# A bilinear feed-forward layer behind a gated linear attention: the second product of pairs of token groups in seven block products instead of eight

## The chip, the cores and the metric

The kernel runs on one core of a Trainium2 chip. The metric is the time on the device in microseconds: the median of three runs, and beside it one profiled execution, whose trace is what the rows below come from. Engines go by the profile's names: PE multiplies matrices (PEld is its loading of weights), DVE and ACT work element by element and can read PSUM, where PE leaves its results, POOL does so in SBUF alone, and SP issues DMAs.

## The reference

Two stages follow each other, all in float32. The first is a recurrence over 768 positions for each of 4 batches x 8 heads, with a head dimension of 48; the second takes its result as 3072 tokens of 384 numbers.

```python
f = 1.0 / (1.0 + np.exp(-f_logit))
for t in range(S):
    state = f[:, :, t, :, None] * state + np.einsum('bhd,bhe->bhde', k[:, :, t], v[:, :, t])
    y[:, :, t] = np.einsum('bhd,bhde->bhe', q[:, :, t], state)
x = y.transpose(0, 2, 1, 3).reshape(B * S, H * D)
a = x @ w_a                  # 3072x384 @ 384x1536
b = x @ w_b
return (a * b @ w_out)       # 3072x1536 @ 1536x384
```

## The kernel before

The work is cut into 8 blocks of 384 tokens, two to a batch. The attention for a block comes as two units of four heads (16 units, `u`), the layer for a block as twelve steps `up` and six steps `down`.

A unit goes through stages that touch several engines. `front(u)` (lines 229 to 256) is ACT's two sigmoids, then DVE's scans over the positions, then the reciprocals, more scans and the products that scale q and k. `scores` (275) is 48 small matmuls on PE and a masked copy by DVE to `at`; `turn` (302) transposes k on PE, and ACT copies the result; `gains` (317) is up to 48 small matmuls, and then DVE's chain of six additions and two scalings that makes the states `st`; `within` (354) and `across` (372) are PE's contributions to the unit's result, which ACT copies to `y` and SP sends into `xT`, the token block in the layout that `up` reads, as five DMAs (line 410). Behind them `across` issues the loads of unit u+3. `slot(u)` (467) strings these together in six stages, with `front(u+1)` between them, so that units overlap.

`up(blk, ft)` (419) makes 128 of the 1536 columns of a and of b for a block: three matmuls each of a 128x128 weight with 384 tokens (L425). `product()` (434) then has ACT copy b to SBUF (L440), and DVE multiply a and b into a tile `ab` (L442). The prologue leaves a product behind by one step, so that it always stands behind the next `up`. `down(blk, part)` (447) is half of the second product for a group of 128 tokens: six of twelve matmuls of a 128x128 piece of ab with 384 columns of `w_out` (L453) into one bank of PSUM; the second half ends with ACT's copy to `o_sb` (L463) and a DMA to the output (L465). PSUM's pool `ps_f` has four banks, which ups and downs share; the attention has its own.

Each engine executes its instructions in the order in which the program writes them. That order is set by the loop at lines 609 to 622: `rest` lists the ups and downs (blocks 0 and 1 are interleaved, later blocks are twelve ups and then six downs), and beside it `queue` holds the stages of the slots with the step at which each is due (lines 602 to 608). A stage that is due is written between the matmuls of a step and its product. In the early steps `end` and `begin` also convert weights that arrive as float64 (lines 169 to 218); `w_out` comes last, and then DVE has no more of that to do.

PE takes a float32 matmul as two records of load and matmul each, so 288 matmuls of L453 show as 576.

Of the kernel before, what the change touches and what calls it, by code (L numbers as in the profile page):

```python
# [10 lines left out]
FP32 = mybir.dt.float32  # L11
# [5 lines left out]
ALU = mybir.AluOpType  # L17
# [3 lines left out]
BLK = 384  # L21
PIECE = 768
# [56 lines left out]
def by_quotients(ctx, tc, q, k, f_logit, v, moe_w_a, moe_w_b, moe_w_out, out, ident, weights, bad):  # L79
# [17 lines left out]
    ab_pool = ctx.enter_context(tc.tile_pool(name="ab", bufs=2 * NFT))  # L97
# [4 lines left out]
    def fixed(shape, name):  # L102
        return fixedp.tile(shape, FP32, tag=name, name=name)
# [198 lines left out]
    def turn(u, spare=False):  # L302

        kf = halves(sets[u % NSET]["k"])
        kT = sb1.tile([128, 2, NC, 128], FP32, tag="kT", name="kT")
        ps = pair(spare)
        for n in range(2):
            for c in range(NC):
                o = n * BLK + c * C
                nc.tensor.transpose(ps[n][:, c * C:c * C + C], kf[:, o:o + C], ident)  # L310
            if spare:
                nc.scalar.copy(kT[:, n].rearrange("s c x -> s (c x)"), ps[n][:, 0:BLK])
        if not spare:
            nc.scalar.copy(kT.rearrange("s n c x -> s n (c x)"), ps_x[:, :, 0:BLK])  # L314
        live[u]["kT"] = kT
# [97 lines left out]
        if u >= NQ:  # L413
            load_unit(u + NSET)

    products = {blk: [] for blk in range(NBLK)}
    factors = []

    def up(blk, ft):

        x, ps = xT[blk], {}
        for nm, w in (("b", w_b), ("a", w_a)):
            ps[nm] = ps_f.tile([128, 512], FP32, tag="f", name="f")[:, 0:BLK]
            for kt in range(NKT):
                nc.tensor.matmul(  # L425
                    ps[nm],
                    lhsT=w[:, kt, ft * 128:ft * 128 + 128],
                    rhs=x[:, kt],
                    start=kt == 0,
                    stop=kt == NKT - 1,  # L430
                )
        factors.append((blk, ps))

    def product():

        if not factors:
            return
        blk, ps = factors.pop(0)
        b_sb = sb2.tile([128, BLK], FP32, tag="b_sb", name="b_sb")
        nc.scalar.copy(b_sb, ps["b"])  # L440
        ab = ab_pool.tile([128, BLK], FP32, tag="ab", name="ab")
        nc.vector.tensor_tensor(ab, ps["a"], b_sb, ALU.mult)  # L442
        products[blk].append(ab)

    results = []

    def down(blk, part):

        tg, half = divmod(part, 2)
        if half == 0:  # L450
            results.append(ps_f.tile([128, 512], FP32, tag="f", name="f")[:, 0:DM])
        for ft in range(half * NFT // 2, (half + 1) * NFT // 2):
            nc.tensor.matmul(  # L453
                results[-1],
                lhsT=products[blk][ft][:, tg * 128:tg * 128 + 128],
                rhs=w_out[:, ft],
                start=ft == 0,
                stop=ft == NFT - 1,
            )
        if half == 0:  # L460
            return
        o_sb = sb2.tile([128, DM], FP32, tag="o_sb", name="o_sb")
        nc.scalar.copy(o_sb, results.pop())  # L463
        r0 = blk * BLK + tg * 128
        nc.sync.dma_start(out=out[r0:r0 + 128], in_=o_sb)  # L465
# [24 lines left out]
    def check_held():  # L490

        n = NU * 3
        fits = fixed([128, NU], "fits")
        some = fixed([128, 2], "some")
# [4 lines left out]
        ps = ps_x  # L499
        nc.tensor.matmul(ps[0:1, 0, 0:1], lhsT=some[:, 0:1], rhs=ones, start=True, stop=True)  # L500
        nc.vector.tensor_scalar(bad, ps[0:1, 0, 0:1], 128.0 * n, None, ALU.is_lt)

    with tc.manual_schedule():
        nc.scalar.preload_act_table_set("sigmoid_and_others")
# [91 lines left out]
        rest += [(down, blk, part) for blk in range(2) for part in range(2 * NTG)]  # L596
        for blk in range(2, NBLK):
            rest += [(up, blk, ft) for ft in range(NFT)] + [(down, blk, part) for part in range(2 * NTG)]
        slots = {s: slot(s) for s in range(2 * NQ, NU + 1)}
        a_block = NFT + 2 * NTG  # L600

        queue = [(2 * NFT - 4 + d, fronts[2 * NQ]) for d in (0, 0.9, 1.8)]
        for s in slots:
            at, pace = (s - 2 * NQ - 2) * a_block / 2 + 2 * a_block - (7 if s < NU else 8.5), 1
            if s < 3 * NQ + 1:
                at, pace = 2 * NFT - 2 + 4.7 * (s - 2 * NQ), 0.5
            queue += [(at + pace * d, slots[s]) for d in (0, 1.2, 2.6, 4, 5.5, 7)]
        queue.sort(reverse=True, key=lambda x: x[0])
        for step, (what, blk, i) in enumerate(rest, 5):
            if what is up:  # L610
                convert(needed(i))
                up(blk, i)
            while queue and queue[-1][0] <= step:
                next(queue.pop()[1], None)
            end(6 + (step - 4))
            product()
            begin(ended[0] + 2)
            if what is down:
                product()
                down(blk, i)  # L620
            if (what, blk, i) == (down, NBLK - 2, 2 * NTG - 1):
                check_held()
        for _, s in reversed(queue):
            next(s, None)
# [357 lines left out]
```

## Time and profile before

| what | us |
|---|---|
| median of three runs | 675.97 |
| lowest and highest of them | 674.87, 677.78 |
| the profiled execution | 675.24 |
| its span, first to last instruction | 673.4 |
| PE busy in the span | 633.0 |
| DVE, ACT, POOL busy | 257.2, 174.3, 66.9 |
| PE in the second product (L453) | 191.0 |
| PE in the two first products (L425) | 203.6 + 204.4 |

A row of a group gives the line, the engine, the operation, out<-in by the program's names, the partitions and elements, and the number of records; behind the first bar the busy time in all and the mean of one in ns, behind the second the idle time of the engine just before them and what ended it. A row of the timeline begins with its start and its length in us. A record of a matmul includes the way through the array, so that records of a stream overlap: their distance, not their length, is what a stream costs.

### The profile page before, as it was taken

The numbers are of one execution on the slowest core, as the hardware profiler recorded it, in microseconds if no ns is written. First come the engines' busy times: TensorE is split into PE (matmuls) and PEld (weight loads), VectorE is DVE, ScalarE is ACT, GpSimd is POOL, SyncE is SP. The second block draws the span as 40 slices with busy tenths as digits, with TensorE's granted clock in tenths as the row PEclk, the third lists the DMA queues.
The fourth block names the chain that finished last, engine by engine and source line by source line (L and its number), as shares of the span: only waits on it lengthen the run. The fifth ranks groups of instructions, "written<-read, shape, count | busy, mean of one in ns | idle before, by whom it ended". The sixth has DMA issues, their size and how long they took to land.

```text
span 673.4 us, 11228 instructions
## 1 busy us (share of the span) xinstructions
PE 633.0 (94%) x4770; PEld 386.6 (57%) x4770; DVE 257.2 (38%) x498; ACT 174.3 (26%) x300; POOL 66.9 (10%) x57
## 2 busy tenths in 40 slices
PE   1577999999999999999999999999999999999996
PEld 1454555556665666656665666556666566555553
DVE  7978899864423143222413125042523111001100
ACT  3565578410221211112211212112121111111100
POOL 6234356110000000000000000000000000000000
PEclk9877999999999999999999999999999999999999
DMA  8698746000134003140303003040031000010000
GB/s 202 169 239 244 207 128 221 1 1 13 37 99 101 1 19 72 33 92 0 89 14 86 28 0 90 23 100 2 21 73 34 16 0 20 19 36 0 1 13 27
DMA packets 30204, 43.29 MB, mean 64 GB/s; under 512 B 3776, under 2 KB 24768, under 8 KB 30144
## 3 DMA queue, kind: packets, MB, share of 16 engines
q1 hardware_dynamic: 29856, 42.19, 23.9%
q8 instruction: 39, 0.64, 0.4%
q10 hardware_dynamic: 288, 0.30, 0.2%
q14 instruction: 21, 0.17, 0.1%
HBM read 33.03 MB, written 4.72 MB: 56 GB/s over the span
## 4 chain that ended last, share of the span: by engine, by line
PE 87%; DVE 4%; DMA 4%; SPq 1%; issue 1%; ACT 1%; POOL 0%; DVEq 0%; ACTq 0%
PE f L425 54%; PE f L453 26%; DMA xT<-y 2%; DMA k_in<-in_k_dram 2%; PE ps_y L363 2%; PE ps_x L283 2%; PE ps_y L384 1%; PE ps_x L329 1%; DVE inv L252 1%; PE ps_x L310 1%; SPq L410 1%; DVE f_in L242 1%; ACT y L396 1%; DMA f_in<-in_f_logit_dram 0%; DVE k_in L254 0%
## 5 line engine op out<-in xcount | busy, mean ns | idle before, releaser
L425 PE MATMUL f<-xT,w_a 128*128 128x384 f32 x576 | 203.6, 490 | 5.6 <-DVE start L247 4.6
L425 PE MATMUL f<-xT,w_b 128*128 128x384 f32 x576 | 204.4, 490 | 2.5 <-DMA xT<-y 2.1
L453 PE MATMUL f<-w_out,ab 128*128 128x384 f32 x576 | 191.0, 489 | 0.0
L425 PEld LDWEIGHTS f<-xT,w_a 128*128 128x128 f32 x576 | 110.1, 191 | 83.2 <-issue 6.4
L425 PEld LDWEIGHTS f<-xT,w_b 128*128 128x128 f32 x576 | 107.3, 190 | 75.8 <-issue 4.4
L453 PEld LDWEIGHTS f<-w_out,ab 128*128 128x128 f32 x576 | 107.7, 190 | 71.8
L442 DVE TENSOR_TENSOR ab<-f,b_sb 128x384 f32<-128x384 f32 x96 | 53.2, 555 | 179.1 <-PE f L425 145.5
L440 ACT COPY b_sb<-f 128x384 f32<-128x384 f32 x96 | 46.0, 479 | 206.7 <-PE f L425 205.8
L237 POOL TENSOR_SCALAR inv<-inv 128x768 f32<-128x768 f32 x16 | 15.4, 959 | 367.8 <-ACT inv L234 367.8
L463 ACT COPY o_sb<-f 128x384 f32<-128x384 f32 x24 | 11.5, 479 | 151.5 <-PE f L453 141.1
L185 POOL TENSOR_SCALAR h<-h 128x768 f32<-128x768 f32 (+1 forms) x20 | 43.0, 2152 | 58.9 <-ACT h L179 58.9
L345 DVE TENSOR_TENSOR st<-st,ps_x 128x96 f32<-128x96 f32 x80 | 20.3, 253 | 63.5 <-PE ps_x L329 47.2
L396 ACT COPY y<-ps_y 48x384 f32<-48x384 f32 (+1 forms) x45 | 21.4, 475 | 66.7 <-PE ps_y L384 63.8
L283 PE MATMUL ps_x<-q_in,k_in 48*64 48x64 f32 x720 | 15.6, 236 | 22.3 <-DVE k_in L254 22.3
L299 DVE TENSOR_TENSOR at<-ps_x,causal 128x768 f32<-128x768 f32 x15 | 14.4, 958 | 57.4 <-PE ps_x L283 57.4
L242 DVE TENSOR_TENSOR_SCAN f_in<-f_in,zero 128x384 f32<-128x384 f32 x32 | 28.8, 942 | 8.7 <-ACT f_in L235 5.4
L283 PEld LDWEIGHTS ps_x<-q_in,k_in 48*64 48x64 f32 x720 | 14.0, 150 | 24.1 <-POOL causal L528 14.1
L252 DVE TENSOR_TENSOR_SCAN inv<-inv,start,zero 128x128 f32<-128x128 f32 x64 | 26.9, 462 | 0.0
L343 DVE COPY st<-ps_x 128x96 f32<-128x96 f32 x8 | 2.0, 256 | 51.4 <-PE ps_x L329 51.4
L314 ACT COPY kT<-ps_x 128x768 f32<-128x768 f32 x12 | 9.6, 798 | 41.7 <-PE ps_x L310 41.7
L182 ACT ACTIVATE bit<-sign 128x768 uint16<-128x768 bf16 (+1 forms) x20 | 19.7, 985 | 0.8
L179 ACT ACTIVATE h<-raw 128x768 f32<-128x768 f32 (+1 forms) x20 | 16.9, 846 | 3.6 <-issue 1.9
(64 smaller groups left out, 304.2 us busy)
## 6 DMA issues: line engine op xcount, KB each, us to landing
f_in<-in_f_logit_dram SPq DMA_DIRECT2D x32, 144.0 KB, 3.1
k_in<-in_k_dram SPq DMA_DIRECT2D x32, 144.0 KB, 3.5
q_in<-in_q_dram SPq DMA_DIRECT2D x32, 144.0 KB, 4.1
v_in<-in_v_dram SPq DMA_DIRECT2D x16, 288.0 KB, 4.5
raw<-in_moe_w_out_dram SPq DMA_DIRECT2D x6, 768.0 KB, 4.4
out_dram<-o_sb SPq DMA_DIRECT2D x24, 192.0 KB, 1.9
raw<-in_moe_w_b_dram SPq DMA_DIRECT2D x5, 768.0 KB, 6.3
raw<-in_moe_w_a_dram SPq DMA_DIRECT2D x5, 768.0 KB, 6.5
```

Source lines behind the costliest of these rows:

```text
L179: nc.scalar.activation(h, hi.bitcast(FP32), AF.Abs, scale=HI_SCALE)
L182: nc.scalar.activation(bit.bitcast(U16).rearrange("p (n two) -> p n two", two=2)[:, :, 1], sgn, AF.Relu, scale=-32768.0)
L185: nc.gpsimd.tensor_scalar(h, h, HI_MAX, None, ALU.min)
L242: nc.vector.tensor_tensor_scan(x[:, c], x[:, c], none, math.exp(MIDDLE), ALU.mult, ALU.add)
L252: nc.vector.tensor_tensor_scan(inv[:, w], inv[:, w], none[:, 0:C], first, ALU.mult, ALU.add)
L283: nc.tensor.matmul(ps[h][SUB * p:SUB * p + SUB, o:o + SUB], lhsT=kf[r, tokens(n, c, p)], rhs=qf[r, tokens(n, c, p)], start=True, stop=True,)
L345: nc.vector.tensor_tensor(st[:, j], before, new, ALU.add)
L396: nc.scalar.copy(y[r:r + rows, :, p], ps[p][e:e + rows, 0:BLK].rearrange("r (o m) -> r o m", m=SUB))
L425: nc.tensor.matmul(ps[nm], lhsT=w[:, kt, ft * 128:ft * 128 + 128], rhs=x[:, kt], start=kt == 0, stop=kt == NKT - 1,)
L440: nc.scalar.copy(b_sb, ps["b"])
L442: nc.vector.tensor_tensor(ab, ps["a"], b_sb, ALU.mult)
L453: nc.tensor.matmul(results[-1], lhsT=products[blk][ft][:, tg * 128:tg * 128 + 128], rhs=w_out[:, ft], start=ft == 0, stop=ft == NFT - 1,)
```

## The change

The 128-token groups of a batch are taken in three pairs: groups 0 and 1 of the even block, its group 2 with group 0 of the odd block, and groups 1 and 2 of the odd block. For a pair, the second product is seen as a product of two matrices of 2x2 blocks: rows are the two groups, the inner dimension of 1536 is cut in two halves of six 128-blocks, and the 384 columns in two halves of 192. It is made by Winograd's form of Strassen's method, seven products of blocks and a number of sums in place of eight products. Four combinations of blocks of `w_out` (t1 to t4) are made once, by DVE, when `w_out` has been converted. Each pair makes four sums of blocks of ab (s1 to s4) on DVE, in tiles that the conversion used before, seven products on PE (P1 to P7, in the order of the code), copies of two partial results on ACT, and five sums of 192 columns with PSUM on DVE. Two results of 192 columns share a bank (x0 and x1, m0 and m1), and waits are kept by tile, so the next writer of one half also waits for the reader of the other.

The tiles `ab` now hold six 128-blocks for the three groups of a block, four tiles in all. A pair's first sum, s3, is written ahead, between earlier steps. The stages of the units are written between the seven products as well, a product counting half a step; their due times are new numbers; `across` moves from behind `gains` to behind `turn`; and the sums of the check on the input (`check_held`) are split off and written ahead.

```diff
     def down(pair):
...
+        s3 = add(block(), a11, a21, ALU.subtract)
+        yield
+        x, m = (ps_f.tile([128, 512], FP32, tag="f", name="f") for _ in range(2))
+        x0, x1, m0, m1 = (t[:, HM * i:HM * i + HM] for t in (x, m) for i in range(2))
+        times(x0, a11, b11, True)
+        u2 = sb2.tile([128, HM], FP32, tag="u2", name="u2")
+        nc.scalar.copy(u2, x0)
+        product()
+        a12, a22 = products[blk0, 1][:, g0], products[blk1, 1][:, g1]
+        s1 = add(block(), a21, a22)
+        s2 = add(block(), s1, a11, ALU.subtract)
+        yield
+        times(m1, s3, t3, True)
+        u3 = sb1.tile([128, HM], FP32, tag="u3", name="u3")
+        nc.scalar.copy(u3, m1)
+        s4 = add(block(), a12, s2, ALU.subtract)
+        yield
+        times(x1, s2, t2)
+        yield
+        times(m0, s1, t1)
+        add(u2, x1, u2)
+        add(u3, u2, u3)
+        yield
+        times(x0, a12, b21)
...
+        add(c22, m0, u3)
+        yield
+        times(m0, s4, b22)
+        nc.scalar.copy(c11, x0)
+        add(c12, m0, u2)
...
+        nc.sync.dma_start(out=out[r0:r0 + 128], in_=o[:, 0])
+        yield
+        times(x1, a22, t4, True)
+        add(c21, x1, u3)
+        nc.sync.dma_start(out=out[r1:r1 + 128], in_=o[:, 1])
+        yield
     def slot(u):
...
         if u < NU:
             turn(u)
+        if u > 2 * NQ:
+            across(u - 1)
         yield
         next(nxt, None)
         yield
         if u < NU:
             gains(u)
-        if u > 2 * NQ:
-            across(u - 1)
         yield
...
-            at, pace = (s - 2 * NQ - 2) * a_block / 2 + 2 * a_block - (7 if s < NU else 8.5), 1
+            at, when = m * a_batch + (-13.4, -0.8, 4.9, 13)[i], (0, 1, 2.2, 2.8, 3.4, 3.9)
...
+            for part in range(7):
+                next(this)
+                if part == 5 and rest[n + 1:] and rest[n + 1][0] is down:
+                    ahead = down(rest[n + 1][2])
+                    next(ahead)
+                step += 0.5
+                if part != 3:
+                    beside()
```

`add` is one `tensor_tensor` on DVE, and `times` six matmuls of a 128x128 block with 192 columns (L483, in the profile of the changed kernel; L478 are the sums of `down`, L462 to L465 the combinations).

More of the change, by code (lines that the diff above doesn't have):

```diff
@@ L414, in across @@
             load_unit(u + NSET)
-    products = {blk: [] for blk in range(NBLK)}
+    HFT = NFT // 2
+    products = {}
     factors = []
@@ L431, in up @@
                 )
-        factors.append((blk, ps))
+        factors.append((blk, ft, ps))
     def product():
@@ L437, in product @@
             return
-        blk, ps = factors.pop(0)
+        blk, ft, ps = factors.pop(0)
         b_sb = sb2.tile([128, BLK], FP32, tag="b_sb", name="b_sb")
         nc.scalar.copy(b_sb, ps["b"])
[L441 to L465, printed above, removed]
+        part, i = divmod(ft, HFT)
@@ new lines, in down, with block, add, times @@
+    def down(pair):
+        (blk0, g0), (blk1, g1) = pair
+        b11, b21, b22 = (w_out[:, HFT * i:HFT * i + HFT, HM * j:HM * j + HM] for i, j in ((0, 0), (1, 0), (1, 1)))
+        t1, t2, t3, t4 = combos
+        a11, a21 = products[blk0, 0][:, g0], products[blk1, 0][:, g1]
+        def block():
+            return sb3.tile([128, PIECE], FP32, tag="h", name="h").rearrange("p (k t) -> p k t", k=HFT)
+        def add(to, x, y, op=ALU.add):
+            nc.vector.tensor_tensor(to, x, y, op)
+            return to
+        def times(to, x, w, first=False):
+            for i in range(HFT):
+                nc.tensor.matmul(
+                    to, lhsT=x[:, i], rhs=w[:, i], start=first and i == 0, stop=i == HFT - 1, skip_group_check=True
+                )
+        s3 = add(block(), a11, a21, ALU.subtract)
[22 more added lines that the diff above has]
+        times(x0, a12, b21)
+        o = sb1.tile([128, 2, DM], FP32, tag="o", name="o")
+        c11, c12, c21, c22 = (o[:, i, HM * j:HM * j + HM] for i in range(2) for j in range(2))
+        add(c22, m0, u3)
[3 more added lines that the diff above has]
+        add(c12, m0, u2)
+        r0, r1 = (blk * BLK + g * 128 for blk, g in pair)
+        nc.sync.dma_start(out=out[r0:r0 + 128], in_=o[:, 0])
[4 more added lines that the diff above has]
+        yield
@@ L498, in check_held @@
         nc.vector.tensor_tensor(some[:, 0:1], some[:, 0:1], some[:, 1:2], ALU.add)
-        ps = ps_x
-        nc.tensor.matmul(ps[0:1, 0, 0:1], lhsT=some[:, 0:1], rhs=ones, start=True, stop=True)
-        nc.vector.tensor_scalar(bad, ps[0:1, 0, 0:1], 128.0 * n, None, ALU.is_lt)
+    def check_held():
+        ps = ps_x[0:1, 0, 0:1]
+        nc.tensor.matmul(ps, lhsT=some[:, 0:1], rhs=ones, start=True, stop=True)
+        nc.vector.tensor_scalar(bad, ps, 128.0 * NU * 3, None, ALU.is_lt)
     with tc.manual_schedule():
```

76 lines of the change are left out of this document (57 added, 19 removed).

## The prediction

> **What bounds the kernel now.** I read the page first (busy shares, then the chain that ended last), then the groups by line, then the waits of PE, then the timeline at four places.
>
> ```profile
> span 673.4 us, 11228 instructions
> PE 633.0 (94%) x4770; PEld 386.6 (57%) x4770; DVE 257.2 (38%) x498; ACT 174.3 (26%) x300; POOL 66.9 (10%) x57
> PE 87%; DVE 4%; DMA 4%; SPq 1%; issue 1%; ACT 1%; POOL 0%; DVEq 0%; ACTq 0%
> PE f L425 54%; PE f L453 26%; DMA xT<-y 2%; DMA k_in<-in_k_dram 2%; PE ps_y L363 2%; PE ps_x L283 2%; PE ps_y L384 1%; PE ps_x L329 1%; DVE inv L252 1%; PE ps_x L310 1%; SPq L410 1%; DVE f_in L242 1%; ACT y L396 1%; DMA f_in<-in_f_logit_dram 0%; DVE k_in L254 0%
> L453 PE MATMUL f<-w_out,ab 128*128 128x384 f32 x576 | 191.0, 489 | 0.0
> ```
>
> The columns of the first two rows are busy time, share and instructions; the third and fourth give the last chain. PE is busy 94% of the span and is 87% of the chain; the second product (L453) alone is 26% of it, and its last column says that PE never idled ahead of one of its 576 records. So a microsecond taken out of L453 is a microsecond of the span, as long as nothing else comes late. DVE has the room for new work (38%).
>
> PE does wait at one kind of place after the start, the beginning of the pairs of blocks, here over the window 205 to 600 us (times, and the longest, behind the total), with the first of the five places beside it:
>
> ```profile
> PE f L425 <- DMA xT<-y: 2.1, 4, 0.6
> PE f L425 <- issue: 0.5, 1, 0.5
> 207.80 1.45 PE L425 MATMUL f<-xT,w_b 128*128 128x384 f32 x4
> 209.85 0.88 PE L425 MATMUL f<-xT,w_b 128*128 128x384 f32 x2 [0.59 <-DMA xT<-y]
> ```
>
> The first product of a new block starts, and stops after four records until xT's last piece has landed.
>
> **What a product of 192 columns takes.** Before, 288 matmuls of 384 columns (two records each, 576). After, 12 pairs x 7 products x 6 = 504 matmuls of 192 columns, 1008 records. The pitch of a record comes from long runs, since the mean of 489 ns overlaps with its neighbours:
>
> ```profile
> 644.02 23.38 PE L453 MATMUL f<-w_out,ab 128*128 128x384 f32 x72
> L453 PE MATMUL f<-w_out,ab x576: 486/486/590, 152.6 to 666.9; 128*128 128x384 f32 x192
> L310 PE MATMUL ps_x<-ident,k_in 128*128 128x128 f32 x72 | 9.8, 273 | 0.0
> L453 PEld LDWEIGHTS f<-w_out,ab x576: 186/190/192, 152.5 to 666.6; 128*128 128x128 f32 x192
> 157.24 0.30 PEld L453 LDWEIGHTS f<-w_out,ab 128*128 128x128 f32 x2
> 157.24 0.59 PE L453 MATMUL f<-w_out,ab 128*128 128x384 f32 x1
> ```
>
> 72 records in 23.38, the last one 0.486: 71 pitches in 22.89, 0.3225 each at 384 columns. The transposes, the nearest row with fewer columns behind the same 128x128 f32 weights, come in 12 groups of six: 9.8 / 12 = 0.817 = 5 pitches + 0.273, so 0.109 at 128 columns. The two points lie on 0.83 ns a column and 2 to 3 ns beside it; 192 columns give 0.1624. The question is the weight load, whose record lasts 0.190, longer than that. In the last two rows a run begins: its first matmul takes 0.59 where others take 0.486, so it waited some 0.105 for its weights, and the second load starts 0.30 - 0.19 = 0.11 after the first. The array is thus taken by a load for about 0.107; the rest of its record is latency. 0.107 is under 0.1624, so I take 0.1624: 1008 x 0.1624 = 163.7 for 576 x 0.3225 = 185.8, **22.1 less**. The bounds: 0.161 (half of the old pitch), and 0.192 (a load must end before the next matmul).
>
> [...]
>
> **What the sums cost.** A pair adds on DVE four sums of 128x768 (s3, s1, s2, s4) and five of 128x192 with an operand in PSUM, on ACT three copies of 192, and drops two copies of 384. Once, `combine_w_out` makes four sums of 1152 columns.
>
> ```profile
> L254 DVE TENSOR_TENSOR k_in<-k_in,inv 128x768 f32<-128x768 f32 x16 | 15.6, 976 | 0.0
> L442 DVE TENSOR_TENSOR ab<-f,b_sb 128x384 f32<-128x384 f32 x96 | 53.2, 555 | 179.1 <-PE f L425 145.5 <-ACT b_sb L440 33.4
> L345 DVE TENSOR_TENSOR st<-st,ps_x 128x96 f32<-128x96 f32 x80 | 20.3, 253 | 63.5 <-PE ps_x L329 47.2 <-PE ps_y L384 13.8
> L463 ACT COPY o_sb<-f 128x384 f32<-128x384 f32 x24 | 11.5, 479 | 151.5 <-PE f L453 141.1 <-issue 10.4
> L314 ACT COPY kT<-ps_x 128x768 f32<-128x768 f32 x12 | 9.6, 798 | 41.7 <-PE ps_x L310 41.7
> 131.12 1.24 DVE L442 TENSOR_TENSOR ab<-f,b_sb 128x384 f32<-128x384 f32 x2
> 139.27 1.13 PE L425 MATMUL f<-xT,w_b 128*128 128x384 f32 x3
> ```
>
> A 768 sum is 0.98; a 192 sum lies between 0.253 (96) and 0.555 (384), 0.36; a copy of 192, from 0.479 and 0.798, is 0.32; a sum of 1152 is 1.4. Per pair DVE gets 4 x 0.98 + 5 x 0.36 = 5.7, beside 84 x 0.1624 = 13.6 of PE, so it is the order and not the load that can hurt.
>
> *combine_w_out* stands on DVE between the two products that the row at 131.12 shows: 4 x 1.4 = 5.6, so the second ends near 137.9. PE needs its bank for the up two further on, which starts at 139.27. Hidden with 1.4 to spare; without that cover its cost is at most 5.6.
>
> *Pairs in batches 1 to 3.* No product is pending there when a down starts: each up's product is issued right behind it, since the first down has called `product` once more and so taken away the lag of one with which the prologue begins. From the last up's end: product 0.2 + 0.56, s1 and s2 0.98 each, so s2 is there at 2.7; PE takes P1 and P2 first, 24 x 0.1624 = 3.9, and P3 asks for s2 only then. P5 waits for DVE's u2 and P6 for c22, each one short sum behind a product that is a whole product (1.95) earlier. I cost these nine pairs at nothing; the slack that hides it is 1.2.
>
> *The first pair of batch 0* is the exception. On PE in program order, before:
>
> ```order
> L453 MATMUL f_1376<-w_out_61,ab_976 128x384
> L363 MATMUL ps_y_111<-at_1280,v_in1_94 48x64 x24
> L283 MATMUL ps_x_110<-q_in2_95,k_in2_96 64x64 x24
> L453 MATMUL f_1376<-w_out_61,ab_1022 128x384
> L453 MATMUL f_1376<-w_out_61,ab_1068 128x384
> ```
>
> and now on PE (f_1294 is x, f_1295 is m, the raw tiles are the combinations of w_out, the h tiles the block sums):
>
> ```order
> L483 MATMUL f_1294<-w_out_61,ab_671 128x192 x6
> L310 MATMUL ps_x_110<-ident_58,k_in1_92 128x128 x6
> L483 MATMUL f_1295<-raw_1184,h_1216 128x192 x6
> L329 MATMUL ps_x_110<-v_in1_94,kT_1311 48x48 x24
> L483 MATMUL f_1294<-raw_1183,h_1309 128x192 x6
> L483 MATMUL f_1295<-raw_1182,h_1307 128x192 x6
> L483 MATMUL f_1294<-w_out_61,ab_1016 128x192 x6
> ```
>
> On DVE at the same place:
>
> ```order
> L446 TENSOR_TENSOR ab_1165<-f_1257,b_sb_1304 128x3x128
> L478 TENSOR_TENSOR h_1307<-ab_671,ab_1016 128x768
> L478 TENSOR_TENSOR h_1309<-h_1307,ab_671 128x768
> L242 SCALAR_TENSOR_TENSOR f_in2_97<-f_in2_97,zero_100 128x384 x2
> L243 TENSOR_TENSOR held_109<-f_in2_97,least_101 128x2
> L478 TENSOR_TENSOR h_1330<-ab_1016,h_1309 128x768
> L343 COPY st_1356<-ps_x_110 128x96
> L345 TENSOR_TENSOR st_1356<-st_1356,ps_x_110 128x96 x5
> L352 TENSOR_SCALAR st_1356<-st_1356,f_in1_93 128x48 x2
> L478 TENSOR_TENSOR u2_1302<-f_1294,u2_1302 128x192
> ```
>
> Before, a down needed nothing of DVE but long-done products; now u2 (last row) stands behind two scans, s4 and the eight steps of the state, and the fifth product on PE (w_out_61,ab_1016) waits for u2, since its bank is the one that u2 reads.
>
> ```profile
> L242 DVE TENSOR_TENSOR_SCAN f_in<-f_in,zero 128x384 f32<-128x384 f32 x32 | 28.8, 942 | 8.7 <-ACT f_in L235 5.4 <-POOL inv L237 3.3
> L329 PE MATMUL ps_x<-v_in,kT 64*48 64x48 f32 x704 | 12.5, 213 | 0.0
> ```
>
> From P1's end. DVE: the product behind ACT's copy of u2 and of b (0.2 + 0.32 + 0.48 = 1.0) ends at 1.6, s1 and s2 at 3.5, two scans at 5.4, held at 5.6, s4 at 6.6, eight steps of 0.25 at 8.6, u2 at 9.0. PE: transposes 0.8, P2 1.95, gains 12.5 x 48 / 704 = 0.85, P3 (s2 is just there) and P4 1.95 each: 7.5. **PE waits 1.5.** In the other two pairs no product is pending and s1 and s2 are under P1: u2 comes in time. The bounds for all waits on sums: 0, and 1.0 in each of twelve pairs with this one's in the first, 12.5.
>
> **What the placing takes away.** `across` now runs with `turn`, ahead of `gains`, and the units are due earlier. Ahead of block 2, before and now:
>
> ```order
> L329 MATMUL ps_x_110<-v_in0_90,kT_1630 48x48 x20
> L384 MATMUL ps_y_111<-q_in2_95,st_1497 48x64 x20
> L453 MATMUL f_1650<-w_out_61,ab_1177 128x384
> ...
> L453 MATMUL f_1650<-w_out_61,ab_1315 128x384
> L425 MATMUL f_1738<-xT_1530,w_b_60 128x384 x3
> ```
>
> ```order
> L384 MATMUL ps_y_111<-q_in2_95,st_1566 48x64 x20
> L483 MATMUL f_1681<-raw_1184,h_1616 128x192 x6
> L329 MATMUL ps_x_110<-v_in0_90,kT_1694 48x48 x20
> L483 MATMUL f_1680<-raw_1183,h_1692 128x192 x6
> L483 MATMUL f_1681<-raw_1182,h_1690 128x192 x6
> L483 MATMUL f_1680<-w_out_61,ab_1165 128x192 x6
> L483 MATMUL f_1681<-w_out_61,h_1749 128x192 x6
> L363 MATMUL ps_y_111<-at_1674,v_in0_90 48x64 x24
> L283 MATMUL ps_x_110<-q_in1_91,k_in1_92 64x64 x24
> L483 MATMUL f_1680<-raw_1185,ab_1165 128x192 x6
> L426 MATMUL f_1876<-xT_1516,w_b_60 128x384 x3
> ```
>
> L384 is the last PE work that xT needs. Six matmuls of 384 stood behind it (3.9 us); now six products and two sections stand there (over 11 us), with the same copies, issues on SP and landing to do, which took
>
> ```profile
> 203.98 1.46 ACT L396 COPY y<-ps_y 128x384 f32<-128x384 f32 x3 [4.78 <-PE ps_y L384]
> 204.97 3.05 SPq L410 DMA_DIRECT2D xT<-y  x5
> 207.43 2.28 DMA xT<-y
> ```
>
> from 203.98 to 207.43 + 2.28 = 209.7, 5.7 us. 5.7 fits under 11, so the five waits go: 2.1 + 0.5 of idle time, and the 0.16 per place that the last record's tail (0.486 - 0.3225) hides, 3.4; I take **3.5 less**. Later batches get more room still. The bounds: nothing, if a wait of the same size comes back, and 3.8. On SP stand 24 output DMAs as before, now two a pair; each waits for c12 or c21 and holds the transfers behind it by less than two products, and none of those is due within that. With these waits gone the next to be late is PE itself.
>
> **The sum.** -22.1 - 3.5 + 1.5 = -24.1. The span goes from 673.4 to 649.3. The profiled execution took 675.24, 1.84 over its span, so it would take 651.1; it lies 0.7 under the median of the runs, 675.97. On the median: **651.9**.
>
> **The rivals.** *The weight load sets the pitch.* If a load of 0.190 has to end before its matmul starts, a record takes 0.192: 1008 x 0.192 = 193.5, 7.7 over the old 185.8; with -3.5 and +1.5 that is 681.7, slower. It decides from 0.187 a record (188.5 / 1008), and is measurable as slower from 0.190. For it: the load's record is longer than the matmul would be, and transposes have one record each where products have two. Against it: 0.109 a record with the same weight tile, and the 0.105 at the start of a run. Chance 0.09, 0.07 of it slower than 0.5%. [...]
>
> *The sums come late everywhere.* The 1.2 of slack falls to contention or to an order that I have misread, each pair waits about 1.0: 651.9 + 11 = 663. For it: P3, P5 and P6 each hang on DVE by less than 2 us, seven products deep, twelve times. Against: DVE has under 6 us of sums in 13.6. Chance 0.15.
>
> *The waits for xT stay*, or move to another block: 651.9 + 3.5 = 655.4. For it: SP issues each piece in 0.6 us and has output DMAs in its way. Against: twice the time. Chance 0.1. That the seven products aren't what runs is ruled out by the rows above (128x192 x6).
>
> **How the numbers follow.** My forecast has 0.64; weight load 0.09, late sums 0.15, xT 0.10, other 0.02. The predicted time is the first case's. Its own range is 648 (no wait at all, and the runs' own spread of some 1 us) to 655. To leave out no more than 2 in 10, the range takes in xT's case and most of the late sums: 648 to 663. 0.5% is about what a measurement of this kernel can tell from no change, 3.4 us. Faster: 0.64 + 0.15 + 0.10 and half of the other, 0.90; slower: 0.07; the same: 0.03.
>
> **What would show it.** In the changed kernel's profile L483's PE rows should sum to about 164 us by pitch, a run of six records taking 5 x 0.162 + 0.326; PEld's share should rise to some 72%; PE's waits should show one for u2 of 1 to 2 us near 160 us, and none for xT after 205 us. A pitch of 0.18 or more makes the prediction wrong; so does a row of PE waiting for L478 twelve times.

## The result, and the profile after

The changed kernel takes **657.31 us**, the median of 4 runs (656.16 to 658.57); the kernel before, run beside it, 676.88 (674.87 to 679.43). The ratio is 0.9709, with a 95% interval of 0.9669 to 0.975. The gain is 19.6 us where 24.1 was forecast: the sign and the mechanism came out, and the time stands in the stated range, 5.4 above the forecast and 2.3 above the forecast's own range of 648 to 655. 0.9 of that is the kernel before, which took 676.88 here and not 675.97. The profiled execution took 657.89, with a span of 656.1.

From the page after: the span, the busy shares, and the two largest groups of the second product's matmuls on PE (busy time, mean of a record, idle time ahead).

```profile
span 656.1 us, 12293 instructions
PE 618.1 (94%) x5202; PEld 446.9 (68%) x5202; DVE 327.7 (50%) x610; ACT 174.9 (27%) x312; POOL 68.9 (10%) x57
...
L483 PE MATMUL f<-raw,h 128*128 128x192 f32 x432 | 73.7, 328 | 0.0
L483 PE MATMUL f<-w_out,ab 128*128 128x192 f32 x288 | 51.1, 327 | 0.9 <-DVE u L478 0.9
```

PE is as full as before, and DVE went from 38 to 50% without getting into the way: one single wait (0.9) stands in the last column. The mean of 327 ns says little, because a record's tail overlaps with the next. The pitch is read from a long run, here two whole pairs of batch 3 in the timeline (start, length, records):

```profile
622.58 2.11 PE L483 MATMUL f<-w_out,ab 128*128 128x192 f32 x12
...
636.23 2.11 PE L483 MATMUL f<-w_out,ab 128*128 128x192 f32 x12
```

Between the two starts lie the 84 records of one pair: 13.65 / 84 = 0.1625 each. That is the forecast's 0.1624.

All of PE's waits over the whole span (total, times, longest):

```profile
PE ps_x L283 <- DVE k_in L254: 22.1, 3, 13.9
PE f L426 <- DVE start L247: 4.6, 1, 4.6
PE f L283 <- DVE k_in L254: 1.7, 1, 1.7
PE ps_y L384 <- DVE st L345: 1.2, 1, 1.2
PE f L426 <- DVE w_a L195: 1.0, 1, 1.0
PE f L483 <- DVE u L478: 0.9, 1, 0.9
PE f L384 <- DVE st L343: 0.4, 1, 0.4
```

No row names xT any more; all but the L483 row belong to the start. The one wait for u2 is where the forecast put it, in the first pair of batch 0, on PE and then on DVE:

```profile
160.49 4.17 PE L483 MATMUL f<-raw,h 128*128 128x192 f32 x24
165.58 2.22 PE L483 MATMUL f<-w_out,ab 128*128 128x192 f32 x12 [0.92 <-DVE u L478]
164.86 0.40 DVE L352 TENSOR_SCALAR st<-st,f_in 128x48 f32<-128x48 f32 x2
165.18 0.35 DVE L478 TENSOR_TENSOR u<-f,u 128x192 f32<-128x192 f32 x1
```

DVE comes to u2 only behind the steps of the state (L352 is the last). The stream of PE loses 1.19 here: 0.92 of idle time, 0.16 by which the last record outlasts its pitch (0.326 - 0.1625), and 0.1 for the first weights.

**Where the time went.** Since the span holds a start that differs from run to run, I cut it at the last wait of the start, that of L425 or L426 for w_a (L195), which ends at 71.54 before and at 74.74 after (the rows of these products begin 0.07 earlier; their first record takes that much longer for its weights, and the cut stands behind it). Behind it PE runs through: 601.87 us before, 581.34 after, 20.5 less. Ahead of it the profiled execution of after is 3.2 longer. All experiments below are compared by this figure, "behind the start", whose repeat is good to 0.1 (first experiment).

The forecast's terms make -22.1 - 3.5 + 1.5 = -24.1 of it. What they miss is seen when the attention's stretches are laid side by side. Before, `turn`, `gains` and `across` of slot 7 in PE's timeline:

```profile
231.63 2.10 PE L425 MATMUL f<-xT,w_a 128*128 128x384 f32 x6
233.57 0.82 PE L310 MATMUL ps_x<-ident,k_in 128*128 128x128 f32 x6
234.22 2.10 PE L425 MATMUL f<-xT,w_b 128*128 128x384 f32 x6
...
243.90 2.10 PE L425 MATMUL f<-xT,w_a 128*128 128x384 f32 x6
245.93 0.69 PE L329 MATMUL ps_x<-v_in,kT 64*48 64x48 f32 x37
...
249.31 2.10 PE L425 MATMUL f<-xT,w_a 128*128 128x384 f32 x6
```

and after, the same stages of the same slot:

```profile
218.81 2.10 PE L426 MATMUL f<-xT,w_a 128*128 128x384 f32 x6
220.74 0.82 PE L310 MATMUL ps_x<-ident,k_in 128*128 128x128 f32 x6
221.49 0.89 PE L384 MATMUL ps_y<-q_in,st 48*48 48x64 f32 x48
222.31 2.20 PE L426 MATMUL f<-xT,w_b 128*128 128x384 f32 x6
224.35 2.10 PE L426 MATMUL f<-xT,w_a 128*128 128x384 f32 x6
226.38 0.74 PE L329 MATMUL ps_x<-v_in,kT 64*48 64x48 f32 x40
227.05 2.20 PE L426 MATMUL f<-xT,w_b 128*128 128x384 f32 x6
229.09 2.10 PE L426 MATMUL f<-xT,w_a 128*128 128x384 f32 x6
```

Six records of the first product follow one another at 1.935 (6 x 0.3225; the first two rows of before are 1.94 apart). Take that as the length of each such product and what is left belongs to the stretch between. Before: `turn` 234.22 - 233.57 = 0.65, `gains` and `across` together 249.31 - 243.90 - 2 x 1.935 = 1.54. After: `turn` and `across` 224.35 - 218.81 - 2 x 1.935 = 1.67, `gains` alone 229.09 - 224.35 - 2 x 1.935 = 0.87. That is 2.54 where there was 2.19: 0.35 more per unit, without a wait in any list. The places are seen in the rows: the product ahead of small matmuls takes 2.03 to the next start and not 1.94, the one behind them is 2.20 long and not 2.10, and the rest, some 0.15 by difference, I put down to an overlap of `gains` and `across` that is gone. The transposes of `turn` have full 128x128 operands and cost none of this (their 0.65 is six records of 0.109), so moving `across` to them made a third stretch of small matmuls where there were two. Eleven units pay it: about 3.6.

So behind the start: -22.05 (matmuls), -3.74 (xT's five waits, by the gaps in the stream), +1.19 (u2), +3.6 (the third stretch) make -21.0; measured is -20.5, and the last 0.5 I can't place. It doesn't hang on `across`: for the kernel with `across` moved back (below) the terms give 577.27, and 577.77 is measured.

### The profile page after: what moved, and what is told of

Read it like the earlier page. It is cut to its first block, busy times and chain, and to the rows that moved or that the text cites. A ratio compares the mean times of both kernels' runs of the same rounds, so it can differ in the third digit from the quotient of the medians.

```text
span 656.1 us, 12293 instructions
## 1 busy us (share of the span) xinstructions
PE 618.1 (94%) x5202; PEld 446.9 (68%) x5202; DVE 327.7 (50%) x610; ACT 174.9 (27%) x312; POOL 68.9 (10%) x57
## 4 chain that ended last, share of the span: by engine, by line
PE 90%; DVE 5%; DMA 2%; ACT 1%; issue 1%; POOL 0%; ACTq 0%; SPq 0%; DVEq 0%
PE f L426 57%; PE f L483 24%; PE ps_x L283 2%; PE ps_y L363 2%; PE ps_y L384 2%; PE ps_x L329 1%; DMA xT<-y 1%; DVE inv L252 1%; PE ps_x L310 1%; DVE f_in L242 1%; PE f L310 1%; DVE k_in L254 1%; DMA f_in<-in_f_logit_dram 0%; DVE h L478 0%; DVE q_in L253 0%
## 5 line engine op out<-in xcount | busy, mean ns | idle before, releaser
L426 PE MATMUL f<-xT,w_a 128*128 128x384 f32 x576 | 203.6, 490 | 5.6 <-DVE start L247 4.6
L426 PE MATMUL f<-xT,w_b 128*128 128x384 f32 x576 | 205.7, 494 | 0.0
L426 PEld LDWEIGHTS f<-xT,w_a 128*128 128x128 f32 x576 | 110.1, 191 | 83.2 <-issue 6.4
L426 PEld LDWEIGHTS f<-xT,w_b 128*128 128x128 f32 x576 | 107.8, 191 | 70.4 <-issue 1.2
L483 PE MATMUL f<-raw,h 128*128 128x192 f32 x432 | 73.7, 328 | 0.0
L483 PEld LDWEIGHTS f<-raw,h 128*128 128x128 f32 x432 | 70.2, 190 | 0.5
L483 PE MATMUL f<-w_out,ab 128*128 128x192 f32 x288 | 51.1, 327 | 0.9 <-DVE u L478 0.9
L483 PEld LDWEIGHTS f<-w_out,ab 128*128 128x128 f32 x288 | 47.4, 190 | 3.0 <-DVE u L478 1.2
L478 DVE TENSOR_TENSOR o<-f,u 128x192 f32<-128x192 f32 x36 | 12.9, 357 | 56.6 <-PE f L483 56.4
L283 PE MATMUL ps_x<-q_in,k_in 48*64 48x64 f32 x720 | 16.2, 238 | 22.1 <-DVE k_in L254 22.1
L283 PEld LDWEIGHTS ps_x<-q_in,k_in 48*64 48x64 f32 x720 | 14.6, 151 | 23.9 <-POOL causal L590 13.9
L483 PE MATMUL f<-raw,ab 128*128 128x192 f32 x144 | 25.7, 328 | 0.0
L483 PE MATMUL f<-w_out,h 128*128 128x192 f32 x144 | 25.4, 326 | 0.0
```

The costliest lines, as they stand in the source:

```text
L283: nc.tensor.matmul(ps[h][SUB * p:SUB * p + SUB, o:o + SUB], lhsT=kf[r, tokens(n, c, p)], rhs=qf[r, tokens(n, c, p)], start=True, stop=True,)
L426: nc.tensor.matmul(ps[nm], lhsT=w[:, kt, ft * 128:ft * 128 + 128], rhs=x[:, kt], start=kt == 0, stop=kt == NKT - 1,)
L483: nc.tensor.matmul(to, lhsT=x[:, i], rhs=w[:, i], start=first and i == 0, stop=i == HFT - 1, skip_group_check=True)
```

## The experiments

Differences of time below are taken from the cut of the profiled executions, "behind the start"; the medians of the runs stand beside them.

**The changed kernel once more.** No edit.

> The changed kernel once more, nothing edited. Theory: of the 6.8 us by which its profiled span (656.1) missed the forecast 649.3, 3.2 arose ahead of 74 us, where PE's granted clock stayed low longer (0.50 and 0.66 in two stretches where before had 0.81 and 1.00), and that is chance: in this profile the point where PE runs through again (74.74 us in the first one) lies anywhere between 71 and 75.5, and the span moves with it, 652 to 657. Rival: the longer start belongs to the changed program; then the point is again within 0.5 us of 74.74, and the span within 0.7 of 656.1.

655.95 us (654.81 to 658.57, 4 runs), ratio 0.9698 (0.9654 to 0.9743). Behind the start 581.28, against 581.34; the start ended at 72.62 and not at 74.74. The same program thus has a start that moves by 2.1, and a rest that doesn't move. Over the 29 runs of the kernel before that lay beside the experiments the spans less 601.9 give starts of 70.2 to 75.7, and over the 8 runs of after the spans less 581.3 give 71.8 to 75.5: the 3.2 of the two profiled executions is no property of the change.

**`across` moved back behind `gains`.**

```diff
         if u < NU:
             turn(u)
-        if u > 2 * NQ:
-            across(u - 1)
...
         if u < NU:
             gains(u)
+        if u > 2 * NQ:
+            across(u - 1)
```

> The changed kernel with across behind gains again, as before the change; all due times as in the changed kernel. Theory: a change between full 128x128 products and the small products of the attention costs PE some 0.33 us, and the change made three stretches of small products per unit out of two in eleven units; so turn shrinks from 1.66 to 0.66, gains with across becomes 1.55, and from the point where PE runs through, the span gets shorter by 11 x 0.33 = 3.6 us, to about 578 us behind that point (581.3 in the changed kernel's first profile). The waits for xT stay away, since the units are due early enough without it. Rival: across behind gains brings the five waits for xT back, 3.7 us, and the time stays the same. Second rival: the sections cost the same in either order, and the 3.6 lie elsewhere: 581.

651.2 us (649.87 to 651.49, 4 runs), ratio 0.9621 (0.9585 to 0.9658): faster than the kernel before, and all its runs lie below those of after (654.81 and more). Behind the start 577.77, 3.57 less. The timeline at the same slot shows the old form:

```profile
218.28 2.10 PE L426 MATMUL f<-xT,w_a 128*128 128x384 f32 x6
220.30 0.69 PE L329 MATMUL ps_x<-v_in,kT 64*48 64x48 f32 x37
...
223.69 2.10 PE L426 MATMUL f<-xT,w_a 128*128 128x384 f32 x6
```

223.69 - 218.28 - 2 x 1.935 = 1.54 again. xT's waits stay away, so these went by the earlier due times and not by moving `across`.

**`across` moved forward in the kernel before**, except in the last slot.

```diff
         if u < NU:
             turn(u)
+            if u > 2 * NQ:
+                across(u - 1)
...
-        if u > 2 * NQ:
+        else:
             across(u - 1)
```

> The kernel before with one edit: across stands behind turn, but in the last slot, where it stays. Theory: the waits of PE for xT after 205 us go (3.7 us by the distance of the records) and the third stretch of small products comes, 11 x 0.33 = 3.6: time within 1 us of before, no row of PE waiting for xT. Rival (what the prediction said): the placing alone gains 3.5 us.

676.7 us (673.75 to 678.94, 10 runs), ratio 0.9996 (0.997 to 1.0021), behind the start 601.78 against 601.87. xT's waits are gone here too, and the third stretch has come: `turn` with `across` 1.66, `gains` alone 0.88. A gain and a cost of about 3.7 each cancel, which is what the move was worth by itself.

**A stretch split at another place.** To see whether the cost hangs on `across` or on the change of kind, the kernel with `across` moved back got its other stretch, `within` and `scores`, taken apart in the nine slots from 7 to 15.

```diff
         if u > 2 * NQ:
             within(u - 1)
+        yield
         if u < NU:
             scores(u)
-        yield
         next(nxt, None)
         yield
```

> The kernel with across moved back, and the stretch of within and scores taken apart in the nine units of the batches behind the first: within alone first, and scores one unit of full products later. No instruction is added or left out. Theory, that each further place at which TensorE goes from full products of 128x128 to the small ones of the attention and back costs 0.33 us whatever the small ones are: 9 x 0.33 = 3.0 us, the span behind the point of running through rises from 577.8 to 580.8, with no new wait in the list. Rival, that the 0.33 belonged to across alone (a wait for its state or for its bank): no change, 577.8. Second rival: scores that come later hold up what follows them, and the figure rises by more than 3.5 with waits named for VectorE.

Behind the start 580.70, 2.93 more, where 3.0 was expected; 655.53 us in one run. The timeline of one unit:

```profile
230.52 2.10 PE L426 MATMUL f<-xT,w_a 128*128 128x384 f32 x6
232.54 0.89 PE L363 MATMUL ps_y<-at,v_in 64*48 64x64 f32 x48
233.36 2.20 PE L426 MATMUL f<-xT,w_b 128*128 128x384 f32 x6
235.40 2.10 PE L426 MATMUL f<-xT,w_a 128*128 128x384 f32 x6
237.43 0.93 PE L283 MATMUL ps_x<-q_in,k_in 48*64 48x64 f32 x48
238.29 2.20 PE L426 MATMUL f<-xT,w_b 128*128 128x384 f32 x6
```

Both small stretches have the longer product on either side, and no wait stands in a bracket. The cost belongs to the change between full and small products, not to `across`. Each such change costs PE time, and the run gives it a price: 2.93 / 9 = 0.33 for the way there and back, the lost overlap of the two kinds of small matmuls included.

**What the weight load allows.** Each matmul of the second product in two of 96 columns, with the weights loaded for each, 2016 records.

```diff
-                nc.tensor.matmul(
-                    to, lhsT=x[:, i], rhs=w[:, i], start=first and i == 0, stop=i == HFT - 1, skip_group_check=True
-                )
+                for c in (0, 96):
+                    nc.tensor.matmul(
+                        to[:, c:c + 96], lhsT=x[:, i], rhs=w[:, i, c:c + 96],
+                        start=first and i == 0 and c == 0, stop=i == HFT - 1, skip_group_check=True
+                    )
```

> The changed kernel with each matmul of the second product in two of 96 columns: 2016 records in place of 1008, same sums, same output. It measures the weight load by itself. Theory: the array takes a load for 0.107 us, which is longer than 96 columns (0.0824 by two rates per column), so the pitch becomes 0.107 and the second product 216 us, 52 more: about 708 in all. Rival one: loads hide wholly and the pitch is 0.0824: 166 us, 2.4 more. Rival two: a load's whole record of 0.190 must end first: 383 us, 219 more.

712.67 us in one run, where about 708 was expected. The pitch, from the timeline:

```profile
677.92 2.84 PE L484 MATMUL f<-w_out,ab 128*128 128x96 f32 x24
680.60 2.84 PE L484 MATMUL f<-w_out,h 128*128 128x96 f32 x24
```

24 records in 2.68: 0.1117 each. By the columns it would be 0.0824 (96 x 0.83 ns + 2.6), so something else sets the pace, at 0.112 and not at the 0.190 of a load's record. A fixed cost of every record it can't be, since 48 small matmuls, each with its load, pass in 0.93 (L283, the rows above): by elimination I put it down to the load of 128x128 weights. The forecast's reading of a load, 0.107 of the array's time and the rest latency, holds within 0.005; 192 columns stand 0.05 above that floor.

**u2 earlier.** The kernel with `across` moved back, and u2's addition right behind its product (from behind P4 to behind P3 in the order of the code; the expectation counts otherwise); the gains of slots 4 to 6, which run beside batch 0's pairs, half a step later, so that DVE comes to it.

```diff
         times(x1, s2, t2)
+        add(u2, x1, u2)
         yield
         times(m0, s1, t1)
-        add(u2, x1, u2)
         add(u3, u2, u3)
...
-                when = ((-1.1, -1.1, 0.5, 0.5, 1, 2.5), ...
+                when = ((-1.1, -1.1, 0.5, 0.5, 1.5, 2.5), ...
```

> The changed kernel with across behind gains again, and the addition of u2 moved from its place behind P6 to a place right behind P3, so that VectorE does it before S3 and not behind S1 and S2; the gains of slots 4 to 6 fall due half a step later. Theory: the 1.19 us for which the first product P5 of batch 0 waits at 160 us goes, and nothing else changes, so that the span behind the point from which TensorE runs through falls from the 577.8 of the kernel with across moved back to 576.6. Rival: the wait isn't for u2 but for VectorE's whole queue, so it stays at about 1.2 and the figure stays at 577.8; a second rival, that u2's earlier addition holds up the combination or the softmax ahead of which it now stands, gives new waits and a figure above 578. The time follows with the start, whose point of running through has been 70.3 to 74.7 us: 649 to 653.

651.14 us (650.45 to 652.03, 5 runs), ratio 0.9613 (0.9586 to 0.964); behind the start 577.65, against 577.77. The wait for u2 went, and another took its place, in PE's timeline:

```profile
155.31 2.12 PE L483 MATMUL f<-raw,h 128*128 128x192 f32 x12
158.15 2.19 PE L483 MATMUL f<-raw,h 128*128 128x192 f32 x12 [0.72 <-DVE h L478]
160.26 0.76 PE L329 MATMUL ps_x<-v_in,kT 64*48 64x48 f32 x48
```

The gains (L329), which used to stand between P2 and P3, had covered the sum S2; moved by half a step they cover it no longer. The wait is for DVE's whole queue in this pair, not for u2's place in it: the expectation's rival.

**Another order of the products.** x0 and x1 are halves of one tile, and P5 writes x0, so it waits for u2's read of x1. Here P5 goes ahead of P3, and S4's product to the end.

```diff
+        times(x0, a12, b21)
+        yield
         times(x1, s2, t2)
+        add(u2, x1, u2)
+        add(u3, u2, u3)
+        nc.scalar.copy(c11, x0)
         yield
         times(m0, s1, t1)
+        add(c22, m0, u3)
+        yield
+        times(x1, a22, t4, True)
...
+        times(m0, s4, b22)
```

> The kernel with across moved back, and the seven products in another order: the second product into x0 (a12 by b21) stands third, then S2 and S1 follow, then a22 into x1, and S4 last. Since x0 and x1 are two halves of one tile, the product into x0 no longer has to wait until u2's addition has read x1, and S2 and S4 have one or two products more of time. Theory, that the 1.19 us at 160 us was a wait for a read of the other half of one tile: it goes, no wait takes its place, and the span behind the point of running through falls from 577.8 to 576.6. Rival, as in the run both, that VectorE is simply late in this pair: a wait of 0.7 to 1.2 turns up at another product and the figure stays at 577.6 to 577.8. Second rival: new waits in many pairs (c22 ahead of S4's product, c11 ahead of a22's), 578 to 582.

655.66 us (653.84 to 657.63, 4 runs), ratio 0.9699 (0.9665 to 0.9733). Behind the start 578.85, 1.1 more than before the edit. No product waits for a sum or for u2 any more, but PE now comes to the scores before DVE has their k_in, at two places of batch 0:

```profile
169.99 0.93 PE L283 MATMUL ps_x<-q_in,k_in 48*64 48x64 f32 x48 [0.27 <-DVE k_in L254]
...
205.06 1.03 PE L283 MATMUL ps_x<-q_in,k_in 48*64 48x64 f32 x48 [1.61 <-DVE k_in L254]
```

So the theory was half right: the wait for the other half of a tile went, and waits for DVE took its place, 1.9 in all where the rival had 0.7 to 1.2. By these two runs DVE sets the pace in batch 0 within a microsecond or two, whichever of its results is asked for first.

**Without the four block sums.** S1 to S4 are replaced by blocks of `ab`.

> The changed kernel without the four sums of blocks of the second product's operand: S1 to S4 are left out and the blocks themselves stand in their places, so the output is another one. The matmuls are the same in number and shape. Theory, that the sums are covered but for the wait of the first P5 (where u2's addition stands behind S1 and S2 on VectorE): the 1.19 us at 164 us goes and nothing else changes, so that the span behind the point of running through falls from 581.3 to 580.1. Rival, sums late or in the way in many pairs: a gain of 5 us or more, 576 or less, and VectorE's busy time falls by about 9 us, 48 operations, in either case.

655.07 us in one run; behind the start 580.06, 1.28 less than after's 581.34, with the wait for u2 gone and nothing else changed. DVE has 48 operations and 45 us less to do (282.6 us busy instead of 327.7; the 9 us that I had expected of them was a slip, 48 x 0.95 is 46), and the kernel gets 1.3 out of it. The sums are as hidden as the forecast had them.

**S1 and S2 twice each.**

```diff
         s1 = add(block(), a21, a22)
+        add(s1, a21, a22)
         s2 = add(block(), s1, a11, ALU.subtract)
+        add(s2, s1, a11, ALU.subtract)
```

> The changed kernel with S1 and S2 each computed twice into the same block, the same result. This lengthens the way from the last operand block to the products that need S1, S2 and S4 by about two operations of VectorE in each pair. Theory, with the slack of the sums taken as 1.2 us in the forecast and the order of VectorE's work: the four pairs that follow a first product without attention work between (one in batch 1, one in batch 2, two in batch 3) wait about 0.8 each, the first pair of batch 0 waits 1.9 more, the three third pairs 0.5 each, the others nothing: in sum about 6.6, a span behind the point of running through of about 588. Rival, the slack is larger than the forecast had it: only the pair of batch 0 waits longer, 582 to 584. Rival, the sums are always last to come: 12 pairs by 1.0 or more, 593 or more.

668.09 us in one run; behind the start 591.17, 9.8 more, where the theory had 6.6. PE's waits behind the start are one row:

```profile
PE f L483 <- DVE h L478: 7.6, 8, 1.9
```

and the first of its eight places in PE's timeline is

```profile
162.83 5.85 PE L483 MATMUL f<-raw,h 128*128 128x192 f32 x24 [1.93 <-DVE h L478]
```

The pairs that wait are the first of batch 0 and the seven named in the expectation, each for S2; the other four don't. In the stream the seven lose 0.79 to 1.57, together 7.3, where 4.7 was expected, so the slack of these seven under 1.95 of added work is 0.4 to 1.2: the 1.2 of the forecast is its upper end. The first pair loses 2.1 and no longer the 1.19 for u2. The rest is a surprise in the row at 162.83: 24 records take 5.85 where they take 4.06. The granted clock says why (columns: window, its length, PE's busy time and records, clock, DMA share, GB/s):

```profile
164.00:166.00 2.00, 2.00 (x8) 0.51 0.00 0
166.00:168.00 2.00, 2.00 (x9) 0.64 0.00 0
```

Behind a wait of 1.93 the clock fell to half for some 3.4 us (by these two windows, (0.49 + 0.36) x 2 / 0.5), and ten records came 0.320 apart in place of 0.1625; with the two at its ends that is 1.7 more. 7.3 + 2.1 - 1.2 + 1.7 = 9.9, against 9.8.

**Work for PE in the start.** The kernel with u2 earlier, and six matmuls more in the second block of the first product, while PE waits for DVE's weights; their results are overwritten.

```diff
+            for kt in range(6 if (blk, ft, nm) == (0, 1, "a") else 0):
+                nc.tensor.matmul(ps[nm], lhsT=w_b[:, kt % NKT, 0:128], rhs=x[:, kt % NKT], start=True, stop=True)
```

> The kernel of the run both, and six further products of 128x128 by 384 columns in the first product's second block at about 48 us, at a time when TensorE waits some 5 us for VectorE's conversion of the weights; their results are overwritten and used by nobody. They keep TensorE at work through that wait. Theory, that the granted clock of the start follows TensorE's own work just before it: fewer records at half rate between 52 and 65 us, and TensorE runs through from 68 to 70 us instead of 70 to 75, so that the span is some 2 us below that of the run both at an equal figure behind that point (576.6). Rival, that the start's clock is chance: the point lies between 70 and 75 as in the other runs, and the span is equal to that of both within 2 us. Third possibility: the start is bound by VectorE's conversions and by the loads, and the point of running through moves by less than 0.5 whatever the clock.

651.94 us (650.42 to 652.07, 4 runs), ratio 0.9627 (0.9597 to 0.9658), no better than without. The granted clock in the start, first of the kernel before (window, length, busy time and records, clock, DMA share, GB/s), then of after, then here:

```profile
52.00:56.00 4.00, 1.90 (x3) 0.59 0.96 250
56.00:60.00 4.00, 3.77 (x53) 0.56 0.84 212
```

```profile
52.00:56.00 4.00, 0.59 (x1) 0.81 1.07 292
56.00:60.00 4.00, 3.77 (x10) 0.50 0.44 108
60.00:64.00 4.00, 4.00 (x56) 0.50 0.92 268
64.00:68.00 4.00, 4.00 (x28) 0.91 0.60 190
```

```profile
52.00:56.00 4.00, 3.35 (x11) 1.00 0.82 208
56.00:60.00 4.00, 1.71 (x55) 1.00 1.02 283
```

with, in this kernel's timeline,

```profile
58.44 1.03 PE L283 MATMUL ps_x<-q_in,k_in 48*64 48x64 f32 x48 [2.29 <-DVE k_in L254]
```

The half rate is gone, and what it took has turned into a wait for DVE's k_in (last row). The start ended at 71.07, against 72.31 in the kernel with u2 earlier, but also against 70.37 in the kernel with `across` moved back, which ran at 0.50 and 0.81 in the same two windows. So PE's clock at 52 to 60 us doesn't by itself set the start's length.

Over the twelve profiled executions the start does go with the mean of the granted clock from 30 to 66 us. It is 0.76 (some 17 us at half rate) in the four whose start ended at 70.0 to 71.5 (before, `across` moved back, `across` forward in before, 96 columns), 0.72 (20 us) in five that ended at 72.3 to 73.3, and 0.67 (24 us) in two that ended at 74.7 and 75.1 (after, S1 and S2 twice); only the run here, 0.86 and 71.07, stands outside. DVE's fourth k_in goes with it almost as well: it ended at 57.2 to 58.5 in the five starts up to 71.5, and at 59.1 to 60.0 in six of the seven later ones, but at 58.4 in the kernel without the block sums, whose start ended at 73.3. Over single runs the mean clock of the whole span doesn't order the times: the kernel before had a span of 677.1 at 0.986 and one of 673.6 at 0.979. Whether a slow clock makes DVE late, or a late DVE leaves PE idle and so slow, isn't shown.

## Why the prediction was right, and what it missed

- **The matmuls, -22.1:** right. 0.1625 a record was measured for 0.1624, and the rival of the weight load is out: with 96 columns the floor that I put down to the load shows at 0.112, far from the 0.187 at which the change would stop paying (by the forecast's own terms that is 187.8 / 1008 = 0.186; it divided 188.5). The transposes that gave the forecast its point at 128 columns have load records of 0.141 and not 0.190, so they alone were no test of that load; the 96 columns are.
- **xT's waits, -3.5:** right, 3.74. The rival that they stay is out. The five places are the starts of blocks 2 to 6, not of pairs of blocks, which changes nothing in the sum.
- **u2 in the first pair of batch 0, +1.5:** right in place and cause, 1.19 in size. The runs with u2 earlier and with another order show that its cover can't be had for nothing: DVE is late there by about as much for whatever comes next.
- **Nine pairs at nothing, with 1.2 of slack, and `combine_w_out` hidden:** right. Leaving the sums out gives 1.28 in all, nearly the one wait; adding 1.95 to each pair makes seven of the nine wait, just those that the run's expectation had named, and puts their slack at 0.4 to 1.2. No wait of PE stands behind `combine_w_out`. The 0.2 that the forecast put between an up's last record and DVE's product is 0.10 in the trace of before (from 644.19 to 644.29).
- **"What the placing takes away":** this is the step that failed; it left the sign as it was and put the time beyond the forecast's own range. It counted the waits that the new places of the stages remove and took the matmuls that were moved as moved for nothing. `across` left `gains` for `turn`, whose transposes are full-sized, and so became a stretch of small matmuls of its own; each of eleven units pays 0.33. The forecast lacks a term of **+3.6**, and that is nearly all of the difference between -24.1 and -20.5. Moving `across` back returned 3.57, splitting another stretch cost 2.93 in nine units.
- **The start at nothing:** true of the programs, since the 110 instructions of DVE and 64 of ACT that start ahead of the cut are the same in kind and order, but a single profiled execution was 3.2 off by it. The range's 1 us for the spread of the runs was too little for one execution.
- **PEld at 72% of the span:** 68%; I had added 432 records of 0.19 in full, and in the busy time records that overlap count once.

That the time lies in the stated range is luck: it missed the forecast's own range of 648 to 655, and the stated one had been stretched to 663 for waits that didn't come.

## What to carry to other kernels

In this kernel a product of fewer columns is worth what its pitch says, read from a long run (0.1625 at 192 columns), as long as it stays above the floor that 96 columns show (0.112), and sums on another engine cost only where that engine is already queued up (here 1.3 us for 45 us of sums). When matmuls are moved, count the places at which full-sized and small products change over, before and after: here each further stretch cost 0.33 us, and no list of waits showed it. Cut a span at the last wait of its start before comparing two single executions, and give the start its own spread.

## What the runs showed of the hardware that was not expected

- A way from products of 128x128 to the small ones of the attention (L283 and L363, L329 and L384) and back cost 0.33 us in this kernel (2.93 for nine, 3.57 for eleven): about 0.09 ahead and 0.10 behind, and by difference 0.14, which I put down to what two kinds of small matmuls overlap when they stand together.
- Behind a wait of 1.93 us (S1 and S2 twice, at 163 us) the granted clock fell to half for some 3.4 us, while waits of 0.92 (after, at 166 us: a clock of 1.00 in the windows from 164 to 168) and 1.61 (the other order, at 205 us) left the records as they are elsewhere, 2.22 for the next twelve. In the start, the half rate behind 52 us lasted (from the windows) some 6.8 us before and 10.2 after.
- Three kernels with `across` moved back (that alone, with u2 earlier, with work in the start) had starts of 70.3 to 72.7 in 13 runs; two more with the same start, the split one with 73.0 in its one run and the one with the products in another order with 73.2 to 77.0 in 4, had later ones, and these two ran on another chip than the three (the kernel before had 71.7 to 74.1 there, no more than elsewhere). Whether this is chance stays open; the version to keep, by its median and by what lies behind the start, is that with `across` moved back, 651.2 us, and the run with u2 earlier can't be told from it.
